# Chunk 1's K, Q and V as casting loads, and a re-ordered opening, in a windowed attention and maxout FFN kernel

## The chip, the cores and the metric

The kernel runs on one core of one Trainium2 chip. The core has TensorE (PE, with PEld for its weight loads), VectorE (DVE), ScalarE (ACT), GpSimd (POOL) and SyncE (SP), which run their own queues in order and wait for each other by semaphores, and 16 DMA engines that all queues share. SP's and POOL's DMAs are two queues of these engines. The metric is the device time of one execution in microseconds (us), the median over several runs.

## The reference

Sliding-window attention with sinks, then a feed-forward layer whose hidden value is the maximum of three products. Cut to what matters:

```python
batch, n_heads, seq, head_dim = (4, 8, 768, 64); n_sink, window = (4, 128)
n_tokens, d_model, d_ff = (3072, 512, 768)

scores = q @ k.T / 8                            # per batch and head
keep = (key < n_sink) | ((query - key >= 0) & (query - key < window))
a = exp(where(keep, scores, -1e9) - max); a = a / sum(a)
x = (a @ v).transpose(0, 2, 1, 3).reshape(3072, 512)
h = maximum(maximum(x @ w1, x @ w2), x @ w3)
out = h @ w_out
```

All inputs and the output are float32. The kernel computes in bf16 with float32 sums.

## The kernel before

Tokens are worked in 12 chunks of 256 (three to a batch). A chunk's attention covers four pairs of heads; a pair is two heads side by side on the 128 partitions. The stages of a chunk, by the names in the code:

- `load` brings K, Q or V of a chunk as float32 on SP's queue (tiles `k_raw`, `q_raw`, `v_raw`), in head halves where `parts=2`. One row of a head and a pair of tokens is 512 B in HBM.
- `cast_qk` casts half a chunk's heads (`g` = 0 or 1) to bf16 and interleaves the heads by pairs; `cast_v` writes V, in four quarters by token half `n` and parity `i`, to the tile `vb`, whose 65th column is one.
- `turn` and `turn2` transpose K or Q on TensorE (four 128x128 transposes for a half of the heads) into a PSUM bank, and copy that to `kT` or `qT`. `turn2` puts K's and Q's halves into one bank.
- `premask` writes the additive mask into a pair's two score banks; `score` adds K Q; `expo` takes the exponential on ScalarE into `e_sb`; `mask` multiplies by 0 or 1 on VectorE where no premask was made.
- `av_open` and `av` multiply by V into the four `o` banks; `norm` divides by the sum (`rc`, `x_sb`, VectorE).
- `xpose` transposes the result (`xT`); `ffn_h` makes 128x512 of the hidden layer with one of the three weights (eight matmuls) and `ffn_max` takes the maximum; `ffn_y` multiplies by `w_out`.
- `sink_k`, `sink_score` and `sink_v` handle the four sink tokens for chunks that don't hold them. Chunk 1 is the first of these.

The weights come as bf16 by GpSimd's queue, which casts them on the way (`load_w`, 256 columns of a weight at a time; `load_wo`).

The order of the work is written out by hand: the body of the kernel is a long list of calls, and each engine runs its instructions in that order. PSUM banks come from a list of eight free ones: `bank` takes the oldest and `give` puts it back at the end, so the order of calls also sets which earlier reader a matmul waits for. Some loads have a `gate`: a small write by GpSimd (`after`, `pool_gate`) into the tile, which holds the load until GpSimd's queue has come to that place. `warm` issues matmuls on zeros at the start.

The opening is what lies ahead of the first long runs of `ffn_h`: chunk 0's attention, chunk 1's attention and the first weights. In it SP issues Q, K, V of chunk 0 and then K, Q, V of chunk 1, all in float32; GpSimd issues each weight load between its own casts.

Of the kernel before, what the change touches and what calls it, by code (L numbers as in the profile page):

```python
# [10 lines left out]
BF16 = mybir.dt.bfloat16  # L11
AF = mybir.ActivationFunctionType
ALU = mybir.AluOpType
# [3 lines left out]
def kernel(  # L17
# [13 lines left out]
    nc = tc.nc  # L31
    B, H, S, D = q.shape
# [9 lines left out]
    CPB = S // 256  # L42
# [6 lines left out]
    with tc.manual_schedule():  # L49
        const = tc.alloc_tile_pool(name="const", bufs=1)  # L50
# [20 lines left out]
        RING = 4  # L71
# [6 lines left out]
        raws, bfs = {}, {}  # L78
# [14 lines left out]
        def load(ci, what="kqv", gate=None, part=None, parts=1, eng=None):  # L93
# [4 lines left out]
            for w in what:  # L98
# [7 lines left out]
                for g in range(parts) if part is None else (part,):  # L106
# [3 lines left out]
                            .rearrange("h (p i) d -> p h (i d)", i=2))  # L110

        def cast_qk(ci, w, g, eng):

            if (ci, w) not in bfs:
                bfs[ci, w] = raw.tile([128, NP, 2, 2, D], BF16, tag=w + "_bf", name=w + "_bf")
            x, y = bfs[ci, w], raws[ci, w]
            f = eng.copy if eng is nc.scalar else eng.tensor_copy
            f(x[:, 2 * g:2 * g + 2].rearrange("q p i a d -> q p a i d"),  # L118
              y[:, 4 * g:4 * g + 4].rearrange("q (p a) i d -> q p a i d", a=2))

        def cast_v(ci, n, i, eng):
            if ci < NEW:
                eng.tensor_copy(  # L123
                    vb[ci % RING][64 * i:64 * i + 64, n, :, 0:D],
                    raws[ci, "v"][64 * n:64 * n + 64, :, i])
                return
            for h in range(2):
                x, y = 64 * h + 32 * i, 64 * n + 32 * h
                eng.tensor_copy(  # L129
                    vb[ci % RING][x:x + 32, n, :, 0:D], raws[ci, "v"][y:y + 32, :, i])  # L130

        def turn(ci, w, g, eng=None):

            pt = bank([128, 4, 128], BF16, "pt")
            x = bfs[ci, w]
            for i in range(4):
                y = x[:, 2 * g + i // 2, i % 2]
                nc.tensor.transpose(pt[:, i], y.rearrange("s a d -> s (a d)"), ident)  # L138
            eng = eng or (nc.scalar if w == "q" else nc.vector)
# [16 lines left out]
        def turn2(ci, w, g, eng=None):  # L156
# [3 lines left out]
            pt = pts[ci, g][:, "kq".index(w)]  # L160
            x = bfs[ci, w]
            for i in range(4):
                y = x[:, 2 * g + i // 2, i % 2]
                nc.tensor.transpose(pt[:, i], y.rearrange("s a d -> s (a d)"), ident)
            eng = eng or (nc.scalar if w == "q" else nc.vector)
# [69 lines left out]

        def factors(x, y):
            for a in range(2):
                nc.gpsimd.tensor_scalar(x[:, a], y, 2.0 ** -30, 1.0, op0=ALU.mult, op1=ALU.add)

# [28 lines left out]
        def sink_init():  # L268
# [6 lines left out]
            for x in ks:  # L275
                nc.gpsimd.memset(x, 0.0)

# [361 lines left out]
        load(0, 'q', part=1, parts=2)  # L639
        warm(8)  # L640
        load(0, 'k')
        load(0, 'q', part=0, parts=2)
        load(0, 'v', part=0, parts=2, gate=pool_gate)
        cast_qk(0, 'q', 1, nc.scalar)
        load(0, 'v', part=1, parts=2)
        masks()
        sink_init()
        factors(msk, addm)
        turn(0, 'q', 1, nc.scalar)
        warm(4)  # L650
        premask(0, (2,))
        cast_qk(0, 'k', 0, nc.scalar)
        cast_qk(0, 'k', 1, nc.vector)
        turn(0, 'k', 1, nc.vector)
        load(1, 'k')
        turn(0, 'k', 0, nc.scalar)
        cast_qk(0, 'q', 0, nc.gpsimd)
        premask(0, (3,))
        score(0, (2,))
        score(0, (3,))  # L660
        turn(0, 'q', 0, nc.vector)
        premask(0, (0,))
        load(1, 'q')
        expo(0, 2)
        cast_v(0, 1, 0, nc.gpsimd)
        cast_v(0, 0, 0, nc.vector)
        cast_v(0, 1, 1, nc.vector)
        cast_v(0, 0, 1, nc.vector)
        load_w(0, 512, 768)
        load(1, 'v')  # L670
        score(0, (0,))
        expo(0, 3)
        cast_qk(1, 'k', 0, nc.gpsimd)
        premask(0, (1,))
# [38 lines left out]
        expo(1, 3)  # L713
        ffn_h(0, 2, 0, 1, nc.vector)
        score(1, (2,))
# [284 lines left out]
```

## Time and profile before

| | |
|---|---|
| runs | 175.75 us median of 3 (175.69 to 176.14) |
| profiled execution: span from first to last instruction | 173.5 us |
| profiled execution: its own whole time | not given on the page; the runs' median is 2.25 us above the span |
| busy share of the span | PE 97%, PEld 74%, DVE 72%, ACT 51%, POOL 63% |
| chain that ended last | PE 93%, DVE 3%, ACT 1% |
| granted TensorE clock | 1.000 |
| DMA | 35.22 MB, mean 203 GB/s |

The page's shares are means over the whole span. A busy TensorE is not a TensorE at its peak, since matmuls are pipelined and their ends are modelled. The chain of waits follows the work that ended last back through what released it, and shows for any stretch which engine decided. A DMA issue is shown when its descriptors are made, not when its data lands; landings are told by the median from issue to landing and by whoever waits for the data.

### The profile page before, as it was taken

What the parts mean: (1) busy time and instruction counts of PE and PEld (TensorE: products, weight loads), DVE (VectorE), ACT (ScalarE), POOL (GpSimd) and SP (SyncE); (2) the same over time, 40 slices, a digit from 0 to 9 for tenths busy, and PEclk for the clock granted to TensorE, in tenths of its full rate; (3) what the DMA queues carried; (4) which work ended last, traced back from release to release, by engine and by line L of the source; (5) the groups of instructions that cost most, each with busy time, mean ns of one, the idle gap of its engine ahead of it and who ended that gap; (6) DMA issues with size and microseconds to landing.
All of it is one profiled execution on the core that took longest, in us unless ns stands there. A gap on an engine that the chain in (4) does not pass through costs nothing.

```text
span 173.5 us, 5418 instructions
## 1 busy us (share of the span) xinstructions
PE 167.7 (97%) x2225; PEld 129.2 (74%) x2225; DVE 125.1 (72%) x262; ACT 88.8 (51%) x183; POOL 110.1 (63%) x193
## 2 busy tenths in 40 slices
PE   7979999999999999999999999999999999999992
PEld 2546889857695697797797797797897896896871
DVE  3187856696697985986877977877778876776361
ACT  4598554587944615817726717627636516510210
POOL 7389507445399999999999999999998700000000
PEclk9999999999999999999999999999999999999999
DMA  4999999999996999988999969969999119017303
GB/s 134 300 289 198 216 217 252 219 274 290 292 210 118 250 264 180 252 188 220 264 186 247 264 165 254 257 163 238 257 176 274 32 34 376 21 35 272 121 2 121
DMA packets 71545, 35.22 MB, mean 203 GB/s; under 512 B 27488, under 2 KB 69984, under 8 KB 71520
## 3 DMA queue, kind: packets, MB, share of 16 engines
q1 hardware_dynamic: 65824, 31.60, 79.0%
q0 software_dynamic: 5552, 3.15, 12.8%
q8 instruction: 17, 0.28, 0.7%
q10 hardware_dynamic: 144, 0.13, 0.2%
q14 instruction: 8, 0.07, 0.1%
HBM read 25.17 MB, written 6.29 MB: 181 GB/s over the span
## 4 chain that ended last, share of the span: by engine, by line
PE 93%; DVE 3%; ACT 1%; issue 0%
PE h_ps L524 55%; PE y_ps L577 11%; PE y_ps L553 7%; PE o L471 7%; PE st L357 3%; PE warm L203 3%; PE st L331 3%; PE pt L138 2%; ACT e_sb L398 1%; PE o L453 1%; DVE x_sb L484 1%; PE sk L423 1%; PE y_ps L599 1%; DVE vb L123 1%; PE xt L496 1%; PE st L311 0%
## 5 line engine op out<-in xcount | busy, mean ns | idle before, releaser
L524 PE MATMUL h_ps<-xT,w 128*128 128x256 bf16 x864 | 101.2, 273 | 0.1
L524 PEld LDWEIGHTS <-w 128*128 128x128 bf16 x864 | 81.9, 98 | 9.9 <-issue 0.3
L540 DVE TENSOR_TENSOR h_sb<-h_sb,h_ps 128x512 bf16<-128x512 bf16 (+1 forms) x74 | 49.3, 671 | 20.0 <-PE h_ps L524 16.0
L536 ACT CAST h_sb<-h_ps 128x512 bf16<-128x512 f32 x35 | 20.5, 585 | 52.2 <-PE h_ps L524 52.2
L129 POOL CAST vb<-v_raw 32x512 bf16<-32x512 f32 x48 | 36.7, 764 | 2.8 <-DMA v_raw<-in_v_dram 0.6
L90 POOL CAST k_bf<-k_raw 32x512 bf16<-32x512 f32 x48 | 29.5, 614 | 2.2
L398 ACT ACTIVATE e_sb<-st 128x512 bf16<-128x512 f32 (+1 forms) x48 | 23.1, 588 | 0.7 <-PE st L331 0.7
L484 DVE TENSOR_TENSOR x_sb<-o,rc 128x256 bf16<-128x256 f32 x48 | 20.4, 424 | 1.6
L577 PE MATMUL y_ps<-wo,h_sb 64*64 64x512 bf16 (+1 forms) x312 | 21.1, 377 | 0.0
L471 PE MATMUL o<-vb,e_sb 128*128 128x65 bf16 x352 | 16.8, 193 | 0.4 <-ACT e_sb L398 0.4
L471 PEld LDWEIGHTS <-e_sb 128*128 128x128 bf16 x352 | 14.6, 97 | 2.8 <-issue 0.8
L123 POOL CAST vb<-v_raw 64x512 bf16<-64x512 f32 x18 | 12.4, 691 | 5.8 <-DMA v_raw<-in_v_dram 5.2
L389 DVE TENSOR_TENSOR e_sb<-e_part,msk 128x1024 bf16<-128x1024 bf16 x16 | 13.5, 865 | 3.1 <-ACT e_part L374 3.0
L406 DVE TENSOR_TENSOR e_sb<-e_sb,msk 128x1024 bf16<-128x1024 bf16 (+1 forms) x18 | 13.3, 756 | 2.1 <-ACT e_sb L398 2.0
L577 PEld LDWEIGHTS <-h_sb 64*64 64x64 bf16 (+1 forms) x312 | 9.9, 106 | 5.0
L374 ACT ACTIVATE e_part<-st 128x384 bf16<-128x384 f32 x32 | 13.1, 496 | 0.5 <-PE st L357 0.5
L553 PE MATMUL y_ps<-wo,h_sb 128*128 128x512 bf16 x54 | 13.0, 380 | 0.0
L481 DVE RECIPROCAL rc<-o 128x4 f32<-128x4 f32 x48 | 8.3, 174 | 3.5 <-PE o L471 3.4
L118 POOL CAST k_bf<-k_raw 128x512 bf16<-128x512 f32 x6 | 3.8, 647 | 9.6 <-DMA k_raw<-in_k_dram 9.4
L553 PEld LDWEIGHTS <-h_sb 128*128 128x128 bf16 x54 | 4.8, 97 | 5.6 <-DVE h_sb L540 0.9
L118 ACT CAST q_bf<-q_raw 128x512 bf16<-128x512 f32 x13 | 7.6, 621 | 2.0 <-DMA q_raw<-in_q_dram 1.9
L427 ACT ACTIVATE e_sink<-sk 128x256 bf16<-128x256 f32 x8 | 3.1, 389 | 10.0 <-PE sk L423 10.0
(90 smaller groups left out, 144.2 us busy)
## 6 DMA issues: line engine op xcount, KB each, us to landing
k_raw<-in_k_dram SPq DMA_DIRECT2D x11, 512.0 KB, 5.7
v_raw<-in_v_dram SPq DMA_DIRECT2D x11, 512.0 KB, 5.8
q_raw<-in_q_dram SPq DMA_DIRECT2D x10, 512.0 KB, 6.5
out_dram<-y_sb SPq DMA_DIRECT2D x9, 512.0 KB, 3.1
w<-in_moe_w_dram POOLq DMA_DIRECT2D x9, 256.0 KB, 6.6
q_raw<-in_q_dram SPq DMA_DIRECT2D x4, 256.0 KB, 7.7
out_dram<-y_sb SPq DMA_DIRECT2D x1, 1024.0 KB, 5.2
wo<-in_moe_w_out_dram POOLq DMA_DIRECT2D x2, 384.0 KB, 7.4
```

What stands on the lines that cost most here:

```text
L90: f(bfs[ci, "k"][x:x + 32, :, n], raws[ci, "k"][y:y + 32, :, i].rearrange("q (p a) d -> q p a d", a=2))
L123: eng.tensor_copy(vb[ci % RING][64 * i:64 * i + 64, n, :, 0:D], raws[ci, "v"][64 * n:64 * n + 64, :, i])
L129: eng.tensor_copy(vb[ci % RING][x:x + 32, n, :, 0:D], raws[ci, "v"][y:y + 32, :, i])
L389: nc.vector.tensor_mul(x.rearrange("q a (t s) c -> q (a t) s c", t=2), y, msk2)
L398: nc.scalar.activation(e[:, a, lo:], st[a][:, lo:], AF.Exp, scale=scale)
L471: nc.tensor.matmul(o[:, t, a], lhsT=e[:, a, s], rhs=vb[cv % RING][:, n, 2 * p + a], start=first, stop=True, skip_group_check=True)
L484: nc.vector.tensor_mul(xs[ci][:, p], o[:, :, :, 0:D], rc.unsqueeze(3).to_broadcast([128, 2, 2, D]))
L524: nc.tensor.matmul(hp[:, f].rearrange("q (i t r) -> q i t r", i=2, r=x.shape[3]), lhsT=w_sb[wi][:, ds, c0:c0 + 128], rhs=x, start=(ds == 0 ...
L536: (nc.scalar.copy if eng is nc.scalar else eng.tensor_copy)(dst, hp)
L540: nc.vector.tensor_max(dst[:, x], dst[:, x], hp[:, x])
L553: nc.tensor.matmul(yp, lhsT=hs[ci][:, fb, t * 128:(t + 1) * 128], rhs=wo[:, fb], start=(fb == 0), stop=(fb == FB - 1))
L577: nc.tensor.matmul(yps[ci][t][c:c + cols], lhsT=hs[ci][hp, fb, x:x + cols], rhs=wo[hp, fb], start=(turn == 0 and fb == 0), stop=(turn == 1 ...
```

## The change

Three things are changed, all in the opening.

1. K, Q and V of chunk 1 are no longer loaded as float32 by SP. `load_bf` loads them on GpSimd's queue straight into bf16 tiles (`k_in`, `q_in`, `v_in`), 128 partitions by 8 heads by 128 values, so a packet reads 512 B and writes 256 B. Their `cast_qk` calls are gone. Since the tile isn't interleaved by pairs, `turned` transposes K and Q head by head: eight transposes with 64 columns of weights and 64 output partitions for four of 128. `cast_v` copies chunk 1's V from the bf16 tile.
2. Chunk 0's K and V are loaded in head halves, the upper half first, without a gate, and V is cast in head halves (eight casts of 64x256, four on GpSimd and four on VectorE, for four of 64x512).
3. The calls are put in another order: the first load of weights is issued behind chunk 1's K and Q, ahead of chunk 0's V casts; V of chunk 1 and the other two thirds of the first weight come after those; the casts of chunk 0's Q, the factors of the mask and the clearing of `ks` go to VectorE; both copies of chunk 1's turned K go to ScalarE; chunk 1's V casts stand behind the xT copies; the first `ffn_h` stands ahead of the sink scores. The warm-up matmuls are 7 and 1 instead of 8 and 4.

In the compiled program lines behind the new functions stand 13 to 16 higher (L123 becomes L145, L524 L540, L484 L500).

```diff
+        def load_bf(ci, w):
+            b, c = divmod(ci, CPB)
+            t0 = c * 256
+            bfs[ci, w] = const.tile([128, H, 2, D], BF16, name=w + "_in")
+            nc.gpsimd.dma_start(
+                out=bfs[ci, w],
+                in_={"k": k, "q": q, "v": v}[w][b, :, t0:t0 + 256]
+                    .rearrange("h (p i) d -> p h (i d)", i=2))
+
+        def turned(pt, ci, w, g):
+            x = bfs[ci, w]
+            for i in range(4):
+                p, j = 2 * g + i // 2, i % 2
+                if x.shape[1] != H:
+                    nc.tensor.transpose(pt[:, i], x[:, p, j].rearrange("s a d -> s (a d)"), ident)
+                    continue
+                for a in range(2):
+                    nc.tensor.transpose(
+                        pt[64 * a:64 * a + 64, i], x[:, 2 * p + a, j], ident)
+
...
-        def cast_v(ci, n, i, eng):
+        def cast_v(ci, n, i, eng, g=None):
+            hh = slice(0, H) if g is None else slice(4 * g, 4 * g + 4)
             if ci < NEW:
+                src = bfs[ci, "v"] if (ci, "v") in bfs else raws[ci, "v"]
                 eng.tensor_copy(
-                    vb[ci % RING][64 * i:64 * i + 64, n, :, 0:D],
-                    raws[ci, "v"][64 * n:64 * n + 64, :, i])
+                    vb[ci % RING][64 * i:64 * i + 64, n, hh, 0:D],
+                    src[64 * n:64 * n + 64, hh, i])
                 return
...
-                nc.gpsimd.memset(x, 0.0)
+                nc.vector.memset(x, 0.0)
...
         load(0, 'q', part=1, parts=2)
-        warm(8)
-        load(0, 'k')
+        warm(7)
+        load(0, 'k', part=1, parts=2)
+        load(0, 'k', part=0, parts=2)
         load(0, 'q', part=0, parts=2)
-        load(0, 'v', part=0, parts=2, gate=pool_gate)
-        cast_qk(0, 'q', 1, nc.scalar)
         load(0, 'v', part=1, parts=2)
+        load(0, 'v', part=0, parts=2)
+        cast_qk(0, 'q', 1, nc.vector)
         masks()
         sink_init()
-        factors(msk, addm)
+        load_bf(1, 'k')
+        load_bf(1, 'q')
+        load_w(0, 512, 768)
         turn(0, 'q', 1, nc.scalar)
-        warm(4)
+        warm(1)
         premask(0, (2,))
+        cast_qk(0, 'k', 1, nc.vector)
+        factors(msk, addm, nc.vector)
+        turn(0, 'k', 1, nc.vector)
         cast_qk(0, 'k', 0, nc.scalar)
-        cast_qk(0, 'k', 1, nc.vector)
-        turn(0, 'k', 1, nc.vector)
-        load(1, 'k')
-        turn(0, 'k', 0, nc.scalar)
-        cast_qk(0, 'q', 0, nc.gpsimd)
         premask(0, (3,))
         score(0, (2,))
         score(0, (3,))
+        cast_qk(0, 'q', 0, nc.vector)
+        turn(0, 'k', 0, nc.vector)
+        expo(0, 2)
         turn(0, 'q', 0, nc.vector)
         premask(0, (0,))
-        load(1, 'q')
-        expo(0, 2)
-        cast_v(0, 1, 0, nc.gpsimd)
-        cast_v(0, 0, 0, nc.vector)
-        cast_v(0, 1, 1, nc.vector)
-        cast_v(0, 0, 1, nc.vector)
-        load_w(0, 512, 768)
-        load(1, 'v')
+        expo(0, 3)
+        for n, i, eng in ((0, 0, nc.gpsimd), (0, 1, nc.vector), (1, 0, nc.gpsimd), (1, 1, nc.vector)):
+            cast_v(0, n, i, eng, 1)
         score(0, (0,))
-        expo(0, 3)
-        cast_qk(1, 'k', 0, nc.gpsimd)
         premask(0, (1,))
         score(0, (1,))
         expo(0, 0)
         expo(0, 1)
-        load_w(0, 256, 512)
+        for n, i, eng in ((0, 0, nc.gpsimd), (0, 1, nc.vector), (1, 0, nc.gpsimd), (1, 1, nc.vector)):
+            cast_v(0, n, i, eng, 0)
+        load_bf(1, 'v')
         av_open(0)
         av(0, 2)
         av(0, 3)
-        turn2(1, 'k', 0, nc.vector)
-        cast_qk(1, 'k', 1, nc.scalar)
+        load_w(0, 256, 512)
+        turn2(1, 'k', 0, nc.scalar)
+        turn2(1, 'k', 1, nc.scalar)
         av(0, 0)
-        cast_qk(1, 'q', 0, nc.gpsimd)
-        cast_qk(1, 'q', 1, nc.scalar)
-        turn(1, 'k', 1, nc.scalar)
+        av(0, 1)
         load_w(0, 0, 256)
-        av(0, 1)
+        turn2(1, 'q', 0, nc.vector)
+        turn2(1, 'q', 1, nc.scalar)
+        sink_k(0)
+        xpose(0, 0, nc.vector, (2, 3, 0, 1))
         premask(1, (0,))
-        turn2(1, 'q', 0, nc.vector)
-        sink_k(0)
+        xpose(0, 1, nc.vector, (2, 3, 0, 1))
+        score(1, (0,))
         premask(1, (1,))
-        turn(1, 'q', 1, nc.scalar)
-        cast_v(1, 0, 0, nc.vector)
-        cast_v(1, 1, 0, nc.vector)
-        load_w(1, 512, 768)
-        xpose(0, 0, nc.vector)
-        score(1, (0,))
         score(1, (1,))
         expo(1, 0)
         expo(1, 1)
+        cast_v(1, 0, 0, nc.vector)
+        cast_v(1, 1, 0, nc.vector)
+        cast_v(1, 1, 1, nc.gpsimd)
+        cast_v(1, 0, 1, nc.gpsimd)
+        load_w(1, 512, 768)
         load_w(1, 256, 512)
-        cast_v(1, 1, 1, nc.gpsimd)
-        xpose(0, 1, nc.vector)
-        cast_v(1, 0, 1, nc.gpsimd)
         load_w(1, 0, 256)
+        ffn_h(0, 2, 0, 1, nc.vector)
         score(1, (3,))
         sink_score(1)
         load(2, 'k', part=0, parts=2, gate=after(0, 300))
         load(2, 'k', part=1, parts=2)
         sink_v(0)
         expo(1, 3)
-        ffn_h(0, 2, 0, 1, nc.vector)
         score(1, (2,))
```

`turn` and `turn2` call `turned` where they had their four transposes, and `factors` takes an engine (GpSimd unless told).

More of the change, by code (lines that the diff above doesn't have):

```diff
@@ L134, in turn @@
             pt = bank([128, 4, 128], BF16, "pt")
[L135 to L138, printed above, removed]
+            turned(pt, ci, w, g)
             eng = eng or (nc.scalar if w == "q" else nc.vector)
@@ L160, in turn2 @@
             pt = pts[ci, g][:, "kq".index(w)]
[L161 to L164, printed above, removed]
+            turned(pt, ci, w, g)
             eng = eng or (nc.scalar if w == "q" else nc.vector)
@@ L234, in masks, with factors @@
             nc.vector.tensor_copy(addm[:, 2:4], addm[:, 0:2])
-        def factors(x, y):
+        def factors(x, y, eng=nc.gpsimd):
             for a in range(2):
-                nc.gpsimd.tensor_scalar(x[:, a], y, 2.0 ** -30, 1.0, op0=ALU.mult, op1=ALU.add)
+                eng.tensor_scalar(x[:, a], y, 2.0 ** -30, 1.0, op0=ALU.mult, op1=ALU.add)
         def masks2():
```

## The prediction

> **What bounds the kernel now.** I read the busy time by stretches first, then the chain of waits, then the DMA queues by stretch, then the opening's instructions in order of time. By stretches (columns: stretch, its length, then busy time of PE, PEld, DVE, ACT, POOL, then granted clock, DMA share, GB/s):
>
> ```profile
> span 173.5 us, 5418 instructions
> 22.00:24.00 2.00, 2.00 (x21) 1.79 (x20) 1.38 (x3) 0.84 (x2) 0.00 (x0) 1.00 1.30 214
> 100.00:120.00 20.00, 20.00 (x315) 16.34 (x316) 15.09 (x29) 9.38 (x21) 18.56 (x30) 1.00 1.00 217
> ```
>
> TensorE is full from about 22 us on, and the change leaves that part's work alone. So it is worth what it takes off, or puts on, the opening. There the chain (start, us, what):
>
> ```profile
> 1.26 3.60 PE warm L203 x8
> 5.29 1.46 PE warm L203 x4
> 7.84 0.35 PE st L331 x4
> 8.20 2.40 ACT e_sb L398 x6
> 10.64 0.36 PE o L471 x6
> 11.24 0.42 DVE x_sb L484
> ...
> 12.21 0.33 DVE kT L171
> ...
> 13.63 0.33 DVE qT L168
> 13.97 0.35 DVE vb L123
> 14.33 0.74 DVE vb L123
> 15.08 0.34 DVE xT L498
> 15.46 0.29 PE sk L423 x4
> 15.88 1.03 PE h_ps L524 x8
> ...
> 17.24 0.34 PE o L453 x8
> ```
>
> First K must land, then chunk 0's scores and exps run, then from 11 to 15.4 us it is VectorE: four norms, and among them a kT copy, a qT copy and two casts of chunk 1's V (1.09 us) ahead of the xT copies. The rows that give durations:
>
> ```profile
> 2.66 0.27 DVE L229 COPY addm<-addm 128x128 bf16<-128x128 bf16 x1 [1.16 <-POOL addm L223]
> ...
> 3.64 0.23 DVE L234 COPY addm<-addm 128x256 bf16<-128x256 bf16 x1
> ...
> 3.99 0.62 ACT L118 CAST q_bf<-q_raw 128x512 bf16<-128x512 f32 x1 [1.68 <-DMA q_raw<-in_q_dram]
> ...
> 5.78 0.43 DVE L118 CAST k_bf<-k_raw 128x512 bf16<-128x512 f32 x1 [1.91 <-DMA k_raw<-in_k_dram]
> ...
> 8.68 0.42 DVE L142 COPY qT<-pt 128x512 bf16<-128x512 bf16 x1 [0.93 <-PE pt L138]
> ...
> 9.03 1.47 DVE L123 CAST vb<-v_raw 64x512 bf16<-64x512 f32 x3
> ...
> 9.17 1.11 POOL L292 DMA_DIRECT2D w<-in_moe_w_dram  x1
> ...
> 10.95 0.75 POOL L292 DMA_DIRECT2D w<-in_moe_w_dram  x1
> ...
> 11.05 0.40 PE L164 MATMUL pt<-ident,k_bf 128*128 128x128 bf16 x4
> ...
> 12.12 0.61 POOL L118 CAST q_bf<-q_raw 128x512 bf16<-128x512 f32 x1 [0.43 <-DMA q_raw<-in_q_dram]
> ...
> 13.82 1.56 POOL L292 DMA_DIRECT2D w<-in_moe_w_dram  x2
> ...
> 14.44 2.06 ACT L398 ACTIVATE e_sb<-st 128x512 bf16<-128x512 f32 x4
> ...
> 15.38 1.28 POOL L123 CAST vb<-v_raw 64x512 bf16<-64x512 f32 x2
> ...
> 15.46 0.29 PE L423 MATMUL sk<-qT,ks 128*32 128x256 bf16 x4 [0.16 <-DVE xT L498]
> ...
> 20.25 1.03 PE L524 MATMUL h_ps<-xT,w 128*128 128x256 bf16 x8
> ...
> 26.87 0.61 POOL L118 CAST k_bf<-k_raw 128x512 bf16<-128x512 f32 x1 [6.94 <-DMA k_raw<-in_k_dram]
> ...
> 28.03 0.39 PE L138 MATMUL pt<-ident,k_bf 128*128 128x128 bf16 x4
> ```
>
> **The change, term by term.** Times after are estimates, the sum of these durations in each engine's new order.
>
> *Start of chunk 0.* VectorE now casts Q's upper heads (3.99 to 4.42), then runs the mask copies (2.66 to 3.87 before: 1.2), two small ks memsets (0.2) and K's cast (0.43): 6.25. Four transposes (0.4, at the slow early clock up to 0.6) and the kT copy (0.42) end at 7.3, so the scores start at 7.4 where they stood at 7.84: 0.45 earlier. The masks now wait behind a DMA, but only premask needs them. ScalarE's cast of Q goes (0.62 against VectorE's 0.43). Then on VectorE: Q's lower cast 0.43, kT 0.42, qT 0.42: 8.6 instead of 9.1. The third and fourth scores follow on TensorE by 9.7.
>
> *V of chunk 0.* Before, the first `o` matmul at 10.64 comes right after the three V casts (9.03 + 1.47 = 10.50; the profile names ScalarE, whose sixth exp ended at 10.60 too, but the banks had been free since the third). Now VectorE casts two head halves first, about 0.25 each (estimate: half the elements of 0.42, plus a fixed part): ready at 9.1, so TensorE's order decides and `o` starts at 9.8, 0.8 earlier.
>
> *K and Q of chunk 1.* ScalarE and GpSimd lose four casts (0.6 each) and VectorE one kT copy, which goes to ScalarE behind the exps. TensorE gets 32 half transposes for 16 whole ones. Upper bound: each of the 16 more costs a whole one's pitch in the row at 11.05, about 0.06 (four in 0.40, of which 0.2 is the last one's own time), +1.0. Lower: 0, since two halves write different columns; L423 shows four matmuls of 256 columns on different columns in 0.29 altogether. I take a third, +0.3, nearest to L423. The walk: `o` for heads 4 to 7 until 10.3, K turns 11.0, `o` for heads 0 to 3 (last exp at 7.75 + 8 x 0.4 = 10.95) 11.5, Q turns 12.4, last norm 12.25.
>
> *xT before V.* After it come two xposes (0.25 each), two premasks (0.43), two scores (0.3): the first `h_ps` at 14.55; then `h_ps` 0.9, score 0.33, `sk` and `sv` 0.35, score 0.33, and `o L453` starts at about 16.5. It waits for `e_sink`: four exps of 0.53 from 13.6, then `sk` done at 16.1, + 0.4: 16.5. Against 17.24 this is **0.7 earlier**. Bounds: 0.3 (half transposes at full price, VectorE with collisions) and 1.1 (no waits on VectorE at all).
>
> VectorE, from the third norm to the first `h` copy, before:
>
> ```order
> L484 TENSOR_TENSOR x_sb<-o,rc 128x256
> L168 COPY qT_74<-pt 128x512
> L123 CAST vb_78<-v_raw 64x8x64 x2
> L498 COPY xT<-xt 128x4x128 x2
> L440 CAST vs_83<-sv 128x130
> L536 CAST h_sb<-h_ps 128x512
> ```
>
> and after:
>
> ```order
> L500 TENSOR_TENSOR x_sb<-o,rc 128x256
> L184 COPY qT_74<-pt 128x512
> L514 COPY xT<-xt 128x4x128 x2
> L145 COPY vb_78<-v_in 64x8x64 x2
> L552 CAST h_sb<-h_ps 128x512
> L456 CAST vs_83<-sv 128x130
> ```
>
> The V casts have moved behind the xT copies, and the first `h` copy ahead of `vs`.
>
> *The DMA.* Packets in one stretch each (9 to 10, 12.5 to 13, 14 to 15, and 32 to 34 us; count, MB, share):
>
> ```profile
> q1 hardware_dynamic: 582, 0.29, 117.3%
> ...
> q0 software_dynamic: 15, 0.01, 11.2%
> ...
> q0 software_dynamic: 395, 0.19, 144.2%
> ...
> q0 software_dynamic: 417, 0.41, 123.8%
> ```
>
> A plain 512 B packet costs an engine 16/582 = 27.5 ns, a casting one (1 KB read, 512 B written) 40.5, one twice as large 77: 4 ns plus 36.4 per KB read. The new casting packets (512 B to 256 B) come to 22 by that line; the other end is 40.5, no cheaper than the ones seen. I take 25, between the line and the plain packet of equal read. The first weight load, issued at 9.17, moved its first packets after 12.5, when SP's queue ran out: 3.4 us. Issued at 3.4, K starts at about 6.9, as SP's 3072 packets for chunk 0 end, so V of chunk 0 lands little later. K and Q then take 1.6 each, done near 10.5, landing near 11.4 (Q: 12.1 before, 11.0 to 13.3 by the bounds). Needed at 11.5.
>
> The Trainium skill (DMA: Bandwidth & Descriptors, Specifications) wants at least 512 B per transfer for full rate and has smaller ones read, modified and written. By that, 256 B writes cost no less than 40.5 ns, Q lands at 13.3 and the forecast becomes the last rival below.
>
> *GpSimd and its queue.* Between the second weight load and the gate of chunk 2's K, before:
>
> ```order
> L292 DMA w_107<-in_moe_w_dram 128x4x256
> L283 COPY ks_81<-kT_69 64x4x4 x2
> L292 DMA w_108<-in_moe_w_dram 128x4x256 x2
> L123 CAST vb_78<-v_raw 64x8x64 x2
> L292 DMA w_108<-in_moe_w_dram 128x4x256
> L615 CAST k_raw<-w_107 1x1
> ```
>
> and after:
>
> ```order
> L308 DMA w_107<-in_moe_w_dram 128x4x256 x2
> L299 COPY ks_81<-kT_69 64x4x4 x2
> L145 COPY vb_78<-v_in 64x8x64 x2
> L308 DMA w_108<-in_moe_w_dram 128x4x256 x3
> L631 CAST k_raw<-w_107 1x1
> ```
>
> All three loads of `w_108` now queue behind copies that wait for V. V is issued after chunk 0's V casts (9.6), its issue takes 0.75 to 1.5 (twice the runs of a weight load), it moves behind the weight load at 12 to 14 and lands at 13.9 to 15.0; the two copies cost up to 1.28, the next issue 0.75. So `w_108` is asked for at 15.8 to 17.0 (13.8 before) and lands at 18.9 to 20.8:
>
> ```profile
> w<-in_moe_w_dram POOLq DMA_DIRECT2D x1, 256.0 KB, 6.1
> ```
>
> which was 13.82 + 6.1 = 19.9. TensorE wanted it at 20.25, now at 19.55. I take a landing at 19.6: stall 0.05, bounds 0 and 1.2. Chunk 2's K is gated 1.2 later; its last turn at 28.03 had 0.55 to spare (cast done at 27.5), and GpSimd's queue ahead of it is emptier by then, so 0, up to 0.5. SP loses three issues and waits earlier at that gate.
>
> **Sum.** −0.7 + 0.05 = −0.65. The profiled span is 173.5; if that execution took the median 175.75, 2.25 lie around it and stay. 173.5 − 0.65 + 2.25 = 175.1.
>
> **Rivals.**
> 1. *No gain.* VectorE's casts and copies at 4 to 7 us now run beside GpSimd's three DMA issues. Before, the issue at 9.17 beside V casts took 1.11 instead of 0.75, and the three casts 1.47 instead of 3 x 0.42. Two such collisions on VectorE's new lead (0.2 each) and the half transposes at full price leave 0.1: 175.65. The Trainium skill (SBUF — State Buffer, SBUF: two separate sides) calls this a lock: a VectorE copy in a two-port mode keeps GpSimd from writing descriptors until it ends. These rows agree in kind; its 620 to 3100 ns is no size seen here.
> 2. *Slower: late first-layer weights.* If `w_108` lands at 20.8, TensorE stalls 1.2 at the fourth `h_ps`, and K of chunk 2, behind it, adds 0.5 at its turn: −0.7 + 1.7 = +1.0, 176.75. Against it: the copies only wait that long if V lands at 15. It decides from a landing at 20.25.
> 3. *Slower: TensorE's clock stays low.* The same 128x512 matmul:
>
> ```profile
> 36.40 2.70 PE y_ps L553 x12
> ```
>
> takes 0.225 there but 0.45 in the first eight `warm`; the rows say clock 1.00 in both, yet the pitch halves only after 5 us of unbroken work. Now 12 become 8, with gaps up to 0.9 before 6.25. If the rise slips by 3 us, some 1.5 of matmuls double: −0.65 + 1.5, 176.6. The Trainium skill (TensorE: Matmul & The Clock Gate, Part 1) has full clock after a busy window of about 3.4 us that starts by itself; by that rule a window here may be missed.
> 4. *Slower: dear small packets.* At 40.5 ns, Q lands at 13.3, TensorE stands 1.8 at its turn: 176.8. The line through the two casting sizes speaks against it.
>
> **Chances.** Main 0.50 (its own range 174.5 to 175.25), no gain 0.20, late weights 0.12, clock 0.08, packets 0.10. A measurement can tell about 0.3% (0.5 us) from no change, so faster 0.5, same 0.2, slower 0.3. From 174.4 (a gain of 1.1 with casting packets at 22 ns, and 0.2 of luck) to 176.8 all but the tails are held.
>
> **What would show it.** Right: first `h_ps` near 14.6, `o L453` near 16.5, Q of chunk 1 landed before 12, no wait of TensorE at the first `w_108` matmul, span 172.9. Wrong: `warm`-like pitch after 6.5, `k_in` packets above 30 ns, GpSimd waiting for `v_in` past 15, or a VectorE cast over 0.6 before 7 us.

## The result, and the profile after

The changed kernel took **178.22 us** (median of four runs, 177.88 to 179.34) where the kernel before took 175.72 in the same session (four runs, 175.32 to 176.14): a ratio of 1.0143, 95% interval 1.0095 to 1.0191. It is slower by 2.5 us. I had forecast 175.1, a range up to 176.8, and half the chance on faster. The profiled execution took 178.51 with a span of 176.8, so 1.7 lie around a span; before's profiled execution must have taken 175.2, half a microsecond less than the median that I set my sum against. Ratios and intervals compare the fast executions of both kernels, while a median is over all, so the two can differ by some tenths of a per cent.

The page of the changed kernel, its span and what the chain of waits is made of (before: 173.5 us, PE 93%, DVE 3%):

```profile
span 176.8 us, 5434 instructions
...
PE 80%; DMA 12%; POOL 3%; SPq 2%; issue 0%; DVE 0%; POOLq 0%
```

TensorE's share of the path fell by 13 points, and transfers and GpSimd took their place. Which ones, the chain shows in order of time (start, us, what):

```profile
3.51 5.54 DMA v_raw<-in_v_dram
...
9.67 0.34 POOL vb L145
10.01 5.79 DMA v_in<-in_v_dram
...
15.85 0.74 POOL vb L145
...
16.63 0.61 POOL vb L145
17.24 2.18 POOL w L308 x3
...
19.46 0.18 POOL k_raw L631
...
20.08 10.47 DMA k_raw<-in_k_dram
...
30.67 0.62 POOL k_bf L138
...
31.34 0.40 PE pt L126 x4
```

Read as one sentence: V of chunk 1 is ordered when GpSimd has cast chunk 0's V, lands at 15.80, GpSimd copies it, only then orders the three pieces of expert 1's weights (2.2 us), only then opens the gate of chunk 2's K, and TensorE waits for that K at 31.34. Before, nothing of this was on the path. TensorE's rows over the same stretch (start, us, instruction, and in brackets the wait ahead of it):

```profile
15.36 1.05 PE L540 MATMUL h_ps<-xT,w 128*128 128x256 bf16 x8
...
17.58 0.29 PE L469 MATMUL o<-vs,e_sink 32*128 32x130 bf16 x8 [0.23 <-DVE vs L456]
...
21.38 1.05 PE L540 MATMUL h_ps<-xT,w 128*128 128x256 bf16 x8 [0.67 <-DMA w<-in_moe_w_dram]
...
26.52 2.79 PE L540 MATMUL h_ps<-xT,w 128*128 128x256 bf16 x24 [1.03 <-DMA w<-in_moe_w_dram]
...
39.66 2.76 PE L569 MATMUL y_ps<-wo,h_sb 128*128 128x512 bf16 x12
```

and in the kernel before:

```profile
17.18 0.41 PE L453 MATMUL o<-vs,e_sink 32*128 32x130 bf16 x8
...
36.34 2.76 PE L553 MATMUL y_ps<-wo,h_sb 128*128 128x512 bf16 x12
```

There are three waits of 0.67, 1.03 and (at 31.34) 0.93 us, 2.63 together, and the sink term `o` stands at 17.58 where it stood at 17.18: 0.40. That makes 3.03 of the 3.3 us by which the span grew; the first `y_ps` starts 3.32 later, and from there to the end both kernels run alike. The other 0.3 lies in how a wait is counted: the profile lets it begin at the modelled end of the matmul ahead of it. From start to start, against the kernel before, the three places are 0.84, 1.21 and 1.09 longer, 3.14 together, and 0.22 comes back in the rows between them.

What the DMA engines did while GpSimd was late, by stretches (columns as in the prediction: stretch, length, busy times, clock, DMA share, GB/s), first in the kernel before, then in the changed kernel:

```profile
17.00:18.00 1.00, 1.00 (x30) 0.70 (x27) 0.79 (x2) 1.00 (x3) 0.96 (x4) 1.00 1.47 194
18.00:19.00 1.00, 1.00 (x18) 0.91 (x15) 0.97 (x3) 0.74 (x2) 1.00 (x2) 1.00 1.45 196
19.00:20.00 1.00, 1.00 (x17) 0.92 (x15) 0.97 (x4) 0.58 (x1) 0.93 (x3) 1.00 1.45 195
```

```profile
17.00:18.00 1.00, 0.77 (x24) 0.52 (x21) 0.53 (x2) 0.99 (x3) 1.00 (x3) 1.00 0.26 35
18.00:19.00 1.00, 1.00 (x23) 0.93 (x20) 0.59 (x1) 1.00 (x3) 1.00 (x2) 1.00 0.53 26
19.00:20.00 1.00, 1.00 (x18) 0.85 (x16) 0.97 (x4) 0.94 (x2) 0.95 (x4) 1.00 0.69 80
```

This is a hole three microseconds wide: the casting queue (GpSimd's) had been emptied while GpSimd stood in a wait, and SP stood at the gate.

### The profile page after: what moved, and what is told of

Its sections match the earlier page's. It is cut to its first block, busy times and chain, and to the rows that moved or that the text cites. A ratio compares the mean times of both kernels' runs of the same rounds, so it can differ in the third digit from the quotient of the medians.

```text
span 176.8 us, 5434 instructions
## 1 busy us (share of the span) xinstructions
PE 167.7 (95%) x2237; PEld 128.3 (73%) x2237; DVE 126.8 (72%) x269; ACT 87.1 (49%) x180; POOL 110.5 (63%) x191
## 4 chain that ended last, share of the span: by engine, by line
PE 80%; DMA 12%; POOL 3%; SPq 2%; issue 0%; DVE 0%; POOLq 0%
PE h_ps L540 48%; PE y_ps L593 10%; PE y_ps L569 7%; DMA k_raw<-in_k_dram 6%; PE o L487 6%; DMA v_in<-in_v_dram 3%; PE st L373 3%; DMA v_raw<-in_v_dram 3%; PE st L347 2%; SPq L107 2%; POOL vb L145 1%; POOL w L308 1%; PE pt L126 1%; PE o L469 1%; PE y_ps L615 1%; PE sk L439 1%
## 5 line engine op out<-in xcount | busy, mean ns | idle before, releaser
L540 PE MATMUL h_ps<-xT,w 128*128 128x256 bf16 x864 | 101.4, 273 | 1.7 <-DMA w<-in_moe_w_dram 1.7
L540 PEld LDWEIGHTS <-w 128*128 128x128 bf16 x864 | 81.8, 98 | 12.0 <-DMA w<-in_moe_w_dram 2.1
L500 DVE TENSOR_TENSOR x_sb<-o,rc 128x256 bf16<-128x256 f32 x48 | 20.4, 424 | 1.6
L145 POOL CAST vb<-v_raw 64x512 bf16<-64x512 f32 (+1 forms) x19 | 11.9, 625 | 5.9 <-DMA v_raw<-in_v_dram 5.2
L405 DVE TENSOR_TENSOR e_sb<-e_part,msk 128x1024 bf16<-128x1024 bf16 x16 | 13.0, 828 | 3.3 <-ACT e_part L390 3.1
L138 POOL CAST k_bf<-k_raw 128x512 bf16<-128x512 f32 x5 | 3.2, 656 | 10.9 <-DMA k_raw<-in_k_dram 10.8
L443 ACT ACTIVATE e_sink<-sk 128x256 bf16<-128x256 f32 x8 | 3.1, 384 | 10.4 <-PE sk L439 10.0
L347 PE MATMUL st<-qT,kT 64*128 64x128 bf16 (+1 forms) x128 | 7.5, 238 | 0.5 <-DVE qT L161 0.3
```

Of the source, the lines that this page charges most:

```text
L145: eng.tensor_copy(vb[ci % RING][64 * i:64 * i + 64, n, hh, 0:D], src[64 * n:64 * n + 64, hh, i])
L500: nc.vector.tensor_mul(xs[ci][:, p], o[:, :, :, 0:D], rc.unsqueeze(3).to_broadcast([128, 2, 2, D]))
L540: nc.tensor.matmul(hp[:, f].rearrange("q (i t r) -> q i t r", i=2, r=x.shape[3]), lhsT=w_sb[wi][:, ds, c0:c0 + 128], rhs=x, start=(ds == 0 ...
```

## The experiments

Each time is a median, each ratio is against the kernel before on the same chip, with its 95% interval. Each diff is against the kernel that its section names.

### 1. Expert 1's weights ahead of the wait

Against the changed kernel:

```diff
         sink_k(0)
+        load_w(1, 512, 768)
+        load_w(1, 256, 512)
+        load_w(1, 0, 256)
         xpose(0, 0, nc.vector, (2, 3, 0, 1))
...
         cast_v(1, 0, 1, nc.gpsimd)
-        load_w(1, 512, 768)
-        load_w(1, 256, 512)
-        load_w(1, 0, 256)
```

> The changed kernel with one edit: GpSimd issues the three loads of the second weight ahead of its two copies of chunk 1's V, in the 3 us in which it stood still for V. Theory A (the casting queue ran dry from 17 to 20 us because those issues waited behind V, and the weight and chunk 2's K came late by it): the hole is gone, the first load of the second weight lands by 19 instead of 21.3, TensorE does not wait for weights, chunk 2's K is asked for near 17.3, and the time falls by 2.5 to 3.3 us, to 175 to 175.7. Theory B (the re-ordered opening or the small casting packets are dear in themselves): the time stays at 177.5 or above.

**176.04** (1.0014, 0.9989 to 1.0039): moving three orders gives back 2.2 of the 2.5 us. So theory A's mechanism holds; the time is 0.3 above its range. The weights are ordered from 13.13 on, the stretches of 17 to 20 us run at 1.43 to 1.45, chunk 2's K is cast at 26.8, and TensorE waits for none of them (a row of GpSimd's, and one of the stretches as above):

```profile
13.13 2.23 POOL L308 DMA_DIRECT2D w<-in_moe_w_dram  x3
...
18.00:19.00 1.00, 1.00 (x25) 0.95 (x22) 0.96 (x3) 0.90 (x2) 1.00 (x2) 1.00 1.43 192
```

One wait is left (the profile is of the fastest of the ten executions, 175.52):

```profile
14.91 1.05 PE L540 MATMUL h_ps<-xT,w 128*128 128x256 bf16 x8
...
17.76 0.29 PE L469 MATMUL o<-vs,e_sink 32*128 32x130 bf16 x8 [0.86 <-DVE vs L456]
```

VectorE's two copies of V wait for its landing at 15.98, and behind them in its queue stand the copy of the first hidden product and the cast of `vs`, which the sink term needs.

### 2. V of chunk 1 by SyncE, in float32

Against the changed kernel:

```diff
         load(0, 'v', part=0, parts=2)
+        load(1, 'v')
...
-        load_bf(1, 'v')
```

> The changed kernel, but chunk 1's V comes as float32 on SP's queue right behind chunk 0's V, and is cast from there; GpSimd's order is else that of the change. Theory A: V lands near 12.5 instead of 15.8, so the issues of the second weight start near 14.5 instead of 17.2 and the hole closes: 175.2 to 176. Theory B: 177.5 or above. If the second weight is early and TensorE still stands, A falls.

**178.68** (1.0142, 1.0084 to 1.0199), far off theory A's forecast. The hole is gone (17 to 22 us at 1.26 to 1.44) and no weight is waited for, so that half held. But V now shares the engines with K and Q of chunk 1 while they move; Q took 9.4 us from order to landing (7.1 in the changed kernel), and TensorE stood at both turns:

```profile
PE pt L129 <- DMA q_in<-in_q_dram: 1.6, 1, 1.6
PE pt L129 <- DMA k_in<-in_k_dram: 0.7, 1, 0.7
```

Its profiled execution, at full clock, took 176.96, so these rows show the fastest of the four; the other three took 178.62 to 178.88, two at a mean clock of 0.990 and one at 0.999, and why they took 1.7 to 1.9 us more isn't shown. V landed sooner here (GpSimd's copies of it start at 13.29, not 15.85), but what that gained was lost on K and Q.

### 3. The kernel before, with the weights late

Against the kernel before:

```diff
-        load_w(1, 512, 768)
         xpose(0, 0, nc.vector)
...
-        load_w(1, 256, 512)
         cast_v(1, 1, 1, nc.gpsimd)
         xpose(0, 1, nc.vector)
         cast_v(1, 0, 1, nc.gpsimd)
+        load_w(1, 512, 768)
+        load_w(1, 256, 512)
         load_w(1, 0, 256)
```

> The kernel before with only the order of GpSimd's queue taken over: the three loads of the second weight behind the two casts of chunk 1's V. V lands at 13.9 there, so the first issue moves from 13.8 to about 15.2. Theory A says the order alone costs nothing as long as the queue holds work, and the first weight's loads fill it until 17: within 0.4 us of before, 175.3 to 176.2. If the place behind the V casts is what costs, whatever the queue holds: 1 us or more slower.

**177.51** (1.0103, 1.0062 to 1.0144): I had called it harmless. The same lateness, without any other part of the change, thins the transfers, less deeply, and makes chunk 2's K late by 0.76:

```profile
17.00:18.00 1.00, 0.97 (x16) 0.45 (x14) 0.49 (x1) 1.00 (x4) 1.00 (x2) 1.00 1.20 99
18.00:19.00 1.00, 1.00 (x24) 0.88 (x24) 0.66 (x2) 1.00 (x3) 0.96 (x4) 1.00 1.06 123
```

The orders stand at 16.05 to 18.3 here, 13.8 to 17.4 in the kernel before. Not all of its loss is explained by that: in its profile the first `o` matmul was 0.4 late already, ahead of the edit, and the sink term 0.55, where the first `y_ps` is 1.96 late. So about 1.4 are left for the late weights.

### 4. Casting loads in the old order

Against the kernel before, with the changed kernel's new functions:

```diff
         sink_init()
+        load_bf(1, 'k')
+        load_bf(1, 'q')
+        load_bf(1, 'v')
         factors(msk, addm)
...
-        load(1, 'k')
...
-        load(1, 'q')
...
-        load(1, 'v')
...
-        cast_qk(1, 'k', 0, nc.gpsimd)
...
-        cast_qk(1, 'k', 1, nc.scalar)
...
-        cast_qk(1, 'q', 0, nc.gpsimd)
-        cast_qk(1, 'q', 1, nc.scalar)
```

> The kernel before in its own order, but chunk 1's K, Q and V come by the casting queue (issued by GpSimd ahead of the mask factors), their casts gone and K and Q turned head by head. Theory A: V is issued near 6 and lands near 13, the queue never runs dry, and VectorE's chain from 11 to 15 us stays: 175 to 176. Theory B (small casting packets or half transposes are dear): above 176.5.

**177.54** (1.0082, 1.0045 to 1.012), theory B's number, but not for its reason. GpSimd's three orders delay its cast of chunk 0's Q, TensorE stands 1.09 at its turn and 0.70 at the first `o`, and then its clock falls:

```profile
11.00:12.00 1.00, 0.52 (x12) 0.55 (x12) 0.43 (x2) 0.74 (x2) 0.96 (x3) 0.82 1.75 178
12.00:13.00 1.00, 1.00 (x18) 0.73 (x15) 0.93 (x4) 0.00 (x0) 0.96 (x4) 0.50 1.43 185
```

There is no hole and no wait for weights: V and the weights are ordered early. The casting loads alone don't pay, for another reason than in the changed kernel. How much the clock adds isn't settled: the ten executions, 176.3 to 180.84, differ by 2 us among those at 0.999 or 1.0 alone.

### 5 to 8. Which of the late things costs what

Run 5, against the changed kernel (run 6 is runs 1 and 5 together):

```diff
         load_w(0, 512, 768)
+        load_bf(1, 'v')
...
-        load_bf(1, 'v')
```

Run 7, against the changed kernel:

```diff
         cast_v(1, 0, 1, nc.gpsimd)
+        load(2, 'k', part=0, parts=2, gate=after(0, 300))
+        load(2, 'k', part=1, parts=2)
         load_w(1, 512, 768)
...
-        load(2, 'k', part=0, parts=2, gate=after(0, 300))
-        load(2, 'k', part=1, parts=2)
         sink_v(0)
```

Run 8, against run 1:

```diff
-        cast_v(1, 0, 0, nc.vector)
-        cast_v(1, 1, 0, nc.vector)
...
         sink_v(0)
+        cast_v(1, 0, 0, nc.vector)
+        cast_v(1, 1, 0, nc.vector)
         expo(1, 3)
```

> The changed kernel with one line moved: GpSimd orders chunk 1's V (bf16) right behind the first piece of expert 0's weights, ahead of its copies of chunk 0's V, and not behind them. The weights of expert 1 stay behind the copies of chunk 1's V. Theory A (the casting queue runs dry because GpSimd stands waiting for V when it should order the weights): V is ordered at about 6.3 us instead of 10.0 and lands at about 14.3 (three transfers of 1,024 packets at 22 to 40 ns on 16 engines stand ahead of it) instead of 15.8, so the weights are ordered at 15.8 to 18.0 instead of 17.2 to 19.4; the hole at 17 to 20 us shrinks by about 1.4 us and the output matmul with the sink term comes 0.4 to 0.8 sooner: 176.2 to 177.0. Rival B (the late landing of V is the whole loss on TensorE, the order of the weights is not): the sink term comes sooner by 0.9 and nothing else moves, 177.3.

> Both at once: chunk 1's V ordered right behind the first piece of expert 0's weights, and expert 1's three pieces ordered ahead of GpSimd's copies of chunk 1's V. Theory A: the first of the two runs above without its hole, and without the 0.86 us that TensorE waited for the sink's values in the run with the weights ahead, since V lands at about 14.3 and VectorE's two copies are over before the first hidden product is there to copy. 176.0 less 0.6 to 0.9: 175.1 to 175.5, so faster than the kernel before by the opening's gain, 0.2 to 0.6. Rival C (what the opening gains is taken back further on, by transfers that set the pace up to the third chunk, whatever the opening does): 175.8 to 176.1, as with the weights ahead alone.

> The changed kernel with the two loads of chunk 2's K, and the write on GpSimd that they wait for, ahead of the three orders for expert 1's weights instead of behind them. It prices the last of the three losses by itself. If the losses add up: the write comes at 17.2 instead of 19.5, K lands at about 28.4 instead of 30.55, the turn of chunk 2's K no longer waits (0.93 us) and the weights are 0.2 later: 177.3 to 177.7. If the loss there is only the same one seen again (TensorE, being ahead, waits for the next late thing): 178.0 to 178.4.

> The run with expert 1's weights ahead, and VectorE's two copies of chunk 1's V moved behind its copies of the hidden product and of the sink's values. Theory A: the sink term no longer waits for V; it comes at about 17.0 instead of 17.76, but the output matmuls behind it need the two copies, which end at about 17.9 instead of 16.9, so that TensorE has some 0.3 to 0.5 us of the wait left: 175.5 to 175.8. Rival C (the opening's gain is taken back further on): 176.0.

Run 5: **177.57** (1.0123, 1.0099 to 1.0148), slower than both forecasts. V was ordered 3.9 us sooner and landed only 1.1 sooner, at 14.7: its time from order to landing went from 5.8 to 8.6, since the one queue has K, Q and a weight to move first. That suffices for the weights (no wait), but their orders still end at 18.2, and the gate behind them costs what it did:

```profile
30.05 0.40 PE L126 MATMUL pt<-ident,k_bf 128*128 128x128 bf16 x4 [1.12 <-POOL k_bf L138]
```

Run 7: **178.87** (1.0188, 1.0146 to 1.0231), no gain at all, and above both forecasts. The gate ahead of the orders saves the wait for K and puts it on the weights, which are later and now share the engines with K:

```profile
22.37 1.05 PE L540 MATMUL h_ps<-xT,w 128*128 128x256 bf16 x8 [1.40 <-DMA w<-in_moe_w_dram]
...
25.30 5.41 PE L540 MATMUL h_ps<-xT,w 128*128 128x256 bf16 x48 [1.43 <-DMA w<-in_moe_w_dram]
```

Runs 5 and 7 speak against three losses that can be mended one by one, and for a single one: everything that GpSimd orders behind V is late, and the order among them only chooses who waits. Runs 6 and 8, **176.07** (1.0053, 1.0016 to 1.0089) and **176.04** (1.0027, 1.0010 to 1.0045), have everything in time and took rival C's number: the sink term's wait of 0.86 was gone, but it stood at 17.47 and 17.65, only 0.29 and 0.11 sooner than in run 1, because the first hidden product ahead of it had become 0.47 and 0.65 later. In run 6 TensorE waited 0.49 for `kT`, 0.27 for K and 0.34 for Q. In run 8 VectorE's four half casts of chunk 0's V took 2.08 us against 1.47 in run 1, though run 8's edit stands behind them: V's order started at 10.21 there and at 10.34 in run 1.

### 9. V ordered where VectorE is idle

The durations of those casts (ns, smallest, median, largest of four) in the changed kernel:

```profile
L145 DVE CAST vb<-v_raw x4: 290/398/746, 9.1 to 10.2; 64x256 bf16<-64x256 f32 x4
```

and in run 1:

```profile
L145 DVE CAST vb<-v_raw x4: 290/334/424, 9.1 to 10.1; 64x256 bf16<-64x256 f32 x4
```

In the changed kernel GpSimd's order of V runs from 10.01 to 10.89, and the cast that starts at 10.24 ends at 10.99. In run 1 the order starts at 10.34, inside the last cast (10.11 to 10.53), which is not stretched. So the cast that started while GpSimd made descriptors was held until 0.1 us after they were made, and the one that had started before them was not; the last section says for which instructions this was seen.

Against run 1, with a gate as an argument of `load_bf` (GpSimd copies the given element into the tile first):

```diff
         turn(0, 'k', 1, nc.vector)
+        load_bf(1, 'v', gate=kT[0][0:1, 0, 2, 0, 0:1])
...
-        load_bf(1, 'v')
```

> The run with expert 1's weights ahead, with one more edit: chunk 1's V is ordered ahead of GpSimd's copies of chunk 0's V, but only once VectorE has written the K of chunk 0's heads 4 to 7 (a copy of one element into V's tile, on GpSimd, waits for it). So V's order, 0.88 us on GpSimd, stands at about 7.4 to 8.3 us, where VectorE waits for TensorE, and no longer beside VectorE's casts of chunk 0's V. Theory D (an order on GpSimd beside a VectorE cast stretches that cast: in seven profiles the last half cast of chunk 0's V took 745 ns where V's order ran beside it, 604 to 612 beside a weight order, and 424 or less where no order did; and V lands too late for the sink's values): the four half casts on VectorE take 1.5 us, not 1.9 to 2.1; V lands at 14.4 to 15.3; the first hidden product starts at 14.9 as with the weights ahead, the sink term at 17.0 instead of 17.76: 175.2 to 175.5. Rival C (TensorE then meets another late thing of the opening): the sink term at 17.4 to 17.7 and 175.8 to 176.1.

**175.65** against 175.80 (0.9985, 0.9964 to 1.0007): level with the kernel before and between the two forecasts. Theory D's parts, as they came:

```profile
7.89 0.88 POOL L118 DMA_DIRECT2D v_in<-in_v_dram  x1 [0.30 <-POOL v_in L117]
8.77 1.77 POOL L147 CAST vb<-v_raw 64x256 bf16<-64x256 f32 x4
...
14.81 1.27 POOL L147 COPY vb<-v_in 64x512 bf16<-64x512 bf16 x2 [0.20 <-DMA v_in<-in_v_dram]
```

V lands at 14.8, the casts on VectorE take 1.63, and the sink term stands at 17.15, between the two forecasts.

### 10. The new opening without casting loads

Against run 1:

```diff
         load(0, 'v', part=0, parts=2)
+        load(1, 'k')
+        load(1, 'q')
+        load(1, 'v')
...
-        load_bf(1, 'k')
-        load_bf(1, 'q')
...
-        load_bf(1, 'v')
+        cast_qk(1, 'k', 0, nc.gpsimd)
         av_open(0)
...
+        cast_qk(1, 'k', 1, nc.scalar)
         turn2(1, 'k', 0, nc.scalar)
         turn2(1, 'k', 1, nc.scalar)
+        cast_qk(1, 'q', 1, nc.scalar)
         av(0, 0)
         av(0, 1)
+        cast_qk(1, 'q', 0, nc.gpsimd)
         load_w(0, 0, 256)
```

> One part of the change alone: the opening re-ordered, chunk 0's K and V by head halves, expert 1's weights ordered ahead of chunk 1's V copies; but chunk 1's K, Q and V come in float32 by SyncE behind chunk 0's V, and GpSimd and ScalarE cast K and Q as the kernel before does. Against the run with the weights ahead it prices the casting loads by themselves. Theory A (three transfers of 1,024 packets, 1.4 us each, stand in the one casting queue ahead of V and the weights, and that is what the opening's gain went into): with them gone from the queue the weights and V come in time, the sink term comes at about 16.7 to 17.0: 175.0 to 175.5. Rival E (the re-ordered opening gains nothing by itself, since chunk 1's K and Q arrive and are cast no sooner): 175.7 to 176.2.

**180.22** (1.0216, 1.0153 to 1.028). Both theories fell; E had the reason nearer, but not its size. In float32 behind chunk 0's V, K of chunk 1 is turned at 12.63 instead of 10.53 and Q at 14.37 instead of 11.95; TensorE stands 2.22 us, and then it runs at half its clock for six:

```profile
10.00:12.00 2.00, 0.41 (x12) 0.29 (x10) 1.48 (x5) 1.02 (x4) 0.24 (x2) 1.00 1.16 315
...
14.00:20.00 6.00, 5.63 (x37) 3.19 (x38) 2.97 (x8) 3.14 (x7) 5.84 (x12) 0.50 1.19 148
```

So the casting loads bring K and Q sooner, and the re-ordered opening lives on that; by run 4 the casting loads alone, in the old order, don't pay either. Each half alone is slower than the kernel before, and both together, with three orders moved (run 1), are within 0.14% of it. That puts the changed kernel's loss on what GpSimd does behind V.

### 11 and 12. What is left of the opening

Run 11, against run 9:

```diff
+        premask(1, (0,))
         turn2(1, 'q', 0, nc.vector)
...
         xpose(0, 0, nc.vector, (2, 3, 0, 1))
-        premask(1, (0,))
```

Run 12, against run 11:

```diff
+        sink_score(1)
         score(1, (3,))
-        sink_score(1)
```

> The run before this one with V's gated order, and one call moved: the mask of chunk 1's first pair of heads (two matmuls of 512 columns, 0.43 us on TensorE, which need nothing but a bank) stands ahead of the turn of chunk 1's Q, where TensorE stood 0.34 us for Q's landing, and no longer between the two transposes of chunk 0's result. Theory D (after the weights, V and the shared stretch on VectorE are mended, what is left of the loss is TensorE's own short waits in the opening): the Q wait goes, the first hidden product starts 0.2 to 0.35 earlier, at 14.7 to 14.85, the sink term at 16.8 to 17.0: 175.3 to 175.5. Rival C (the path to the sink term then runs over VectorE's norms, which end at 12.99 either way): no gain, 175.5 to 175.8; with a new wait for a bank, 175.8 to 176.1.

> The run before this one, and one call moved: the sink scores of chunk 1 stand on TensorE ahead of the scores of its fourth pair of heads, not behind. In the run before, the sink term waited 0.56 us for a bank: its fourth bank comes free with the first exponential of the fourth pair, which stands on ScalarE behind the sinks' exponential (0.38 us), and that waited for the sink scores at 16.25. Theory D: the sink scores are done 0.33 earlier, the sinks' exponential and the next one follow, the sink term stands at 16.9 instead of 17.20: 174.8 to 175.0. Rival C (VectorE's copies of the hidden product and of the sink's values, over at 17.16, then set the sink term): no gain, 175.1 to 175.4.

Run 11: **175.17** against 175.73 (0.9978, 0.9953 to 1.0004), below both forecasts. The first hidden product came at 14.65, but rival C's bank wait came with it: `o` waited 0.56 and stood at 17.20. What was gained came behind it, where the next transposes no longer waited 0.19. Run 12: **175.13** against 175.50 (0.9973, 0.9952 to 0.9995), rival C's number. The bank wait is gone; the sink term stands at 17.08, not 16.9, because VectorE's copies of V took 1.79 beside GpSimd's orders and copies (0.92 in the changed kernel):

```profile
14.45 1.79 DVE L147 COPY vb<-v_in 64x512 bf16<-64x512 bf16 x2 [0.16 <-DMA v_in<-in_v_dram]
16.16 0.67 DVE L554 CAST h_sb<-h_ps 128x512 bf16<-128x512 f32 x1
16.76 0.28 DVE L458 CAST vs<-sv 128x130 bf16<-128x130 f32 x1
```

This version, the change with four pieces of its order mended, is about 3 us faster than the change (by the two ratios to the kernel before, 0.9973 and 1.0143) and 0.27% faster than the kernel before, which is at the edge of what the runs can tell.

## Why the prediction was wrong, and where it was right

| | forecast | measured |
|---|---|---|
| scores of chunk 0 start | 7.4 | 7.41 |
| first `o` | 9.8 | 10.06 |
| last norm of chunk 0 ends | 12.25 | 13.29 |
| first `h_ps` | 14.55 | 15.36 |
| sink term `o` | 16.5 | 17.58 |
| V of chunk 1 lands | 13.9 to 15.0 | 15.80 |
| first piece of expert 1's weights ordered | 15.8 to 17.0 | 17.24 |
| waits for weights | 0.05 (0 to 1.2) | 1.70 |
| wait for chunk 2's K | 0 (up to 0.5) | 0.93 |

**The step that failed is "GpSimd and its queue".** It saw that all three loads of `w_108` queue behind copies that wait for V, and had them asked for at 15.8 to 17.0 and landed at 18.9 to 20.8. That allows 3.1 to 3.8 us from order to landing, for which it gave no row: the 6.1 beside it was taken where the queue was full, and only reckons the landing of the kernel before. Then it chose "a landing at 19.6: stall 0.05" near the good end of its range and "so 0, up to 0.5" for chunk 2's K. The runs put 2.2 us in its place (run 1). Three things were missing. V took 5.79 us from order to landing, not the 4.3 to 5.4 that I had from its issue at 9.6: in run 5, ordered 3.9 sooner, it landed only 1.1 sooner, so the queue and not the order's time set this. The first piece was ordered at 17.24 and took 4.1 to land, and with the queue run empty the engines moved at most 80 GB/s until 20. And the loss came three times, at the first piece of the weights (0.67, inside my bound of 1.2), at the next (1.03) and at K (0.93), since each was ordered behind the last; the forecast had nothing for the next piece, and only rival 2 added K to the first. Rival 2 named the mechanism and gave it 0.12 and 176.75; it happened at 1.5 us above that price.

In the span, term by term: the opening was to give 0.7 and cost 0.40; the weights and K were to cost 0.05 and cost 2.92 (the 3.14 less the 0.22 above). So 3.3 were added where 0.65 were to go.

**"V of chunk 0" and "xT before V" were too good.** I gave each of VectorE's half casts 0.25, half of the 0.42 of a whole one; the first of the four took 0.29, those beside a GpSimd cast up to 0.42, the one beside V's order 0.75, 1.93 in all. That made the norms 1.0 late and `h_ps` 0.8 late, and is the collision that rival 1 had, at another place than it looked: at 4 to 7 us VectorE was held in three instructions (0.85 for the cast of Q instead of 0.43, 0.57 and 0.53 for two mask copies) and the scores still began on time. Two of the signs that I had named for being wrong were there, a VectorE cast over 0.6 before 7 us (0.85) and GpSimd waiting for `v_in` past 15 (15.80). And I wrote that the first `h` copy now stands behind the V copies on VectorE, but charged `o` nothing for V landing late: 0.86 in run 1, once the weights were mended.

**Right were** the start of the scores, the turns of K (10.53) and Q (11.66), that neither waits, and the two disputed prices. The casting packets, in the stretch of 9 to 10 us (count, MB, share):

```profile
q0 software_dynamic: 710, 0.18, 181.0%
```

16/710 is 22.5 ns, the low end of my bounds (22, from the line through the larger packets; the other end was 40.5), so rival 4 was false. The Trainium skill (DMA: Bandwidth & Descriptors, Specifications) wants at least 512 B for full rate, and I had drawn from it that a write of 256 B costs as much as one of 512 B: here it doesn't, at 22.5 ns against 40.5. Sixteen half transposes took 0.57 from the first to what follows (10.53 to 11.10), eight whole ones 0.45 (6.91 to 7.36 before), so 0.24 more for K and Q together where I took 0.3. (Q's took 0.57 in run 1 as well, but 0.80 in the changed kernel, 11.66 to 12.46; why isn't known.) Rival 3 was false for this kernel: its four runs had a mean clock of 0.998 to 1.0.

**Some sums don't come out as written.** Half transposes at full price cost 1.0, so 0.7 more than the 0.3 that I took, which uses up the whole gain of 0.7; the lower bound of 0.3 and the 0.1 of rival 1, which both charge collisions besides, don't follow from that. K and Q end at 6.9 + 2 x 1.6 = 10.1, not 10.5; the landing at 11.4 fits the 10.1. And the 2.25 around a span were 1.7.

## What to carry to other kernels

An engine that both orders transfers and works on their data must give its orders before any work that waits: the price of a late order is not only the wait, but everything behind it in that engine's queue and the transfers that an empty queue doesn't move meanwhile (here three microseconds at 26 to 80 GB/s instead of 195). Where such a queue is moved behind a wait, look for all who are ordered after it and add their waits; bounding each alone hides the sum. When one order is mended, look for the next late thing before counting the gain: runs 5, 6, 7 and 8 each mended what the profile named, and against the kernel that it edited run 5 gained some 0.2% and the others nothing.

## What the runs showed of the hardware

- **GpSimd's order can hold VectorE.** In the changed kernel the orders of `k_in` (3.36 to 4.46), `q_in` (4.47 to 5.37), the first weights (5.35 to 6.11) and `v_in` (10.01 to 10.89) each held one VectorE instruction, which ended 0.0 to 0.22 us after the order. In ten profiles of kernels with `k_in`'s order at 3.36 to 4.46, VectorE's cast of Q began anywhere from 3.83 to 4.07 and the next instruction always at 4.60 or 4.61. VectorE's rows in the changed kernel:

```profile
3.83 0.85 DVE L138 CAST q_bf<-q_raw 128x512 bf16<-128x512 f32 x1 [2.33 <-DMA q_raw<-in_q_dram]
4.60 0.17 DVE L245 COPY addm<-addm 128x128 bf16<-128x128 bf16 x1
...
4.80 0.57 DVE L247 COPY addm<-addm 128x128 bf16<-128x128 bf16 x1
...
5.64 0.53 DVE L250 COPY addm<-addm 128x256 bf16<-128x256 bf16 x1
```

  The same work (the cast and the copies at 4.80 and 5.64) takes 0.43, 0.18 and 0.23 us where no order runs. Held were copies and casts from SBUF to SBUF. Not held were those that began in the first 0.2 us of an order (the copies at 4.60 and 4.70; in run 4 the cast of K at 5.84, 0.43 us, in an order from 5.65 on), nor copies out of PSUM: in run 9 V's order ran from 7.89 to 8.77, and a copy in the middle of it took its usual time:

```profile
8.27 0.43 DVE L170 COPY kT<-pt 128x512 bf16<-128x512 bf16 x1 [0.16 <-PE pt L128]
```

  The Trainium skill (SBUF — State Buffer, SBUF: two separate sides) has an exclusive lock on the port pair that VectorE, in its two-port modes, shares with GpSimd; whichever of the two starts first keeps it for a whole instruction. The rows with a held instruction agree.
- **TensorE's clock fell after stands in the opening, but not after each.** In run 10's profile TensorE stood for 2.22 us from 10.4 on, and the granted clock was 0.50 from 14 to 20 us; all four executions had a mean clock of 0.977 to 0.990. In run 4's profile it stood for 1.09 and 0.70, and the clock was 0.50 from 12 to 15 us; the mean clock of the ten executions ranged from 0.981 to 1.0. In run 2's profile it stood for 0.67 and 1.55 and kept its clock, while two of the other three executions had 0.990. The changed kernel's stands of 0.67 to 1.03 us between 20 and 32 us left it at 1.00. That the stands are the reason fits the order in time, but no run tested it, and where the limit lies wasn't measured.
